# Loads that wait for a softmax, another way of joining float64 words, and a new step list

## The chip, the cores and the metric

The kernel runs on one core of one Trainium2 chip. The metric is the device time of one execution in microseconds (us). The core's engines are TensorE (PE, matmuls and transposes; its weight loads are PEld), VectorE (DVE), ScalarE (ACT), GpSimd (POOL), and SyncE (SP), which here issues every DMA.

## The reference

An attention over a small state is followed by two feed-forward layers. All inputs are float64 or float32 arrays as numpy draws them; the kernel is given the large weights as float64 words, which it makes into float32 itself.

```python
# x: 4 x 8 x 512 x 64, state: 4 x 8 x 32 x 64
a = softmax(x @ state^T / 8);   xread = a @ state
a2 = softmax(state @ x^T / 8);  sread = a2 @ x
x = concat(xread, sread)                       # 4 * 544 = 2176 tokens, 512 wide
x = (x @ w_a) * (x @ w_b) @ w_out              # 512 -> 1536 -> 512
h = x @ w_in                                   # 512 -> 2048
out = softplus(h) @ w_out2                     # 2048 -> 512, softplus = max(h,0) + log1p(exp(-|h|))
```

## The kernel before

The program is recorded first and placed afterwards. Each helper (`copy`, `tt`, `ts`, `stt`, `reduce`, `activation`, `transfer`, `Products`) adds a step to a `Plan`, with the engines that may run it and a cost for each. `Plan.run` reads the table `ORDER`, which gives steps their ranks; `Plan.go` then walks a model of the engines' time, takes for each engine that is free the first step by rank whose inputs are there, gives it places in the pools `F`, `R`, `K` (float32, float32r and PSUM tiles of 512 columns), and issues it. So the rank and the costs together set the order on every engine. Where TensorE would have a gap in that model during the first 60 us, `go` puts small matmuls on zeros into it (`warm`, line 572 of the profile); 14 such matmuls stand at the very start as well.

Attention comes first. Inputs `x` of batch b arrive in two DMAs of 512 KB (`load_x`), are transposed on TensorE (`turned`, line 560), and give scores against the state (`scores_of`, `scores_direct`). `state_softmax(b)` turns scores into weights over the 32 state rows. The first weights are not multiplied with `xread` but with the state first (`state_w`, `state_rows`): `gates_of(s, b)` then multiplies the softmax with that product for 256 columns of w_a and w_b (part s of six), and `y_part(s, b)` applies part s of w_out. The second feed-forward layer follows with `w_in`, softplus and `w_out2`.

A float32 product is carried on TensorE as three float32r products (`Products.three`): both operands are split into a high and a low part (`split_to`), one copy and one subtract each.

Weights arrive as float64 words and are joined to float32 in `convert_to`: `high` is the upper half of each word, `low` the lower one. Before the change this is one ACT and five DVE instructions on [128, 512] or [128, 1024] values: an ACT copy with a scale, a shift (`ts`), a join of the sign (`stt`), a mask that keeps the exponent (`ts`), the low half times that power of two (`stt`) and a float32 add (`tt`). `load_first` brings the first 256 columns of w_a and w_b in two halves each, `load_to` the later units in the order of the list `order`: `("wo", 0)`, `("ab", 1, 0)`, `("ab", 1, 2)`, `("wo", 1)` and so on. SP issues DMAs in program order, and one that waits holds those behind it.

Of the kernel before, what the change touches and what calls it, by code (L numbers as in the profile page):

```python
# [13 lines left out]
ALU = mybir.AluOpType  # L14
# [139 lines left out]


ORDER = """
1 0 3-4 6 18 5 7 17 30 10 19 13 29 20 8 31 22 9 32 21 33 12 23 214 34 11 24 215 14 35 59 25
60 216 61 39 217 37 2 62 38 69 40 16 26 63 15 36 41 133 28 70 64 91 27 42 71 43 47 134 72
128 44 92 45 73 46 65 79 48 129 67 135 80 49 81 136 50 89 68 82 137 126 51 138 74 90 52 55
53 66 75 54 127 83 139 57 77 56 84 108 93 76 130 140 78 109 85 131 58 94 110 156 96 95 111  # L160
87 157 141 100 86 112 142 97 143 98 113 88 132 114 101 144 116 99 102 115 117 103 145 172
118 104 146 106 173 185 147 107 186 119 183 174 236 120 184 190 175 233 121 187 122-123 237
176 188 150 189 124 158 234 258 191 259 125 247 177-178 162 159 179 192 163 193 260 160 248
261 194 149 151 238 168 165 195 161 264 219 196 201 249 164 218 166 105 240 152 197 167 265
154 182 180 155 153 235 198 220 304 250 181 170 199 171 227 207 262 200 202 239 251 290-291
263 335 252-254 242 228 241 208 221 306 203 307 224 204 223 209 222 225 293 305 210 243 205
255 206 169 244 256 309 266 308 245 294 232 336 211 267 310 229 257 270 311 337 268-269 230
212 246 296 275 213 297 322 321 338 271 226 312 272-274 339 298 276-277 313 315 340 379 314
278 284 341 299 350 316-318 343 300 319-320 279 380 342 371 351 302 324 468 280 325 285 292
301 281 344-345 352 148 372 282 353 469 373 303 382 295 358 286 381 354 374 287 357 327 385  # L170
288 329 355 386 328 470 331 347 383 356 360 346 384 330 323 471 417 333 361 363 387 348 472
366 375 473 407-408 231 401 364 477 367 289 326 332 349 475 418 283 334 376 410 402 478 474
404 359 362 476 498 479-482 365 483 409 405 499 377 388 411 368 378 415 500 462 369 505 403
370 501 406 392 446 433 432 502 506 389 412 438 390 413 439 503 419 393 414 395 435-436 396
441 463 391 504 586 464 442 434 587 448 536 588 449 537 440 451 423 443 420 428 397 444 421
589 445 590 422 452 429 465 579 425 437 484 430 416 485 595 585 431 487 591 596 399 398 488
507 426 454-455 394 427 450 447 457 453 594 490 400 597 491 424 466 510-511 494 512-513
598-599 516-518 458 519 493 526 486 527 529 467 530 523 600 524 520 489 460 508 534 461 509
495 538 496 616 541-543 615 514 497 547 551 532 580 593 552 521 554 456 581 555 622 539 560
617 563 561 531 557 565 623 558 568 533 569 571 573 572 574 583 525 540 546 515 618 566 582  # L180
703 556 492 619 528 559 553 522 562 535 575 459 564 620 545 621 592 601-602 548 604-605
607-608 577 610-611 640 567 576 584 570 654 578 549 544 550 704-705 629 609 733 624 603 606
627-628 630 709 706-707 634-635 651 637-638 708 612-613 643-644 625 646-647 614 712 669 626
641 653 713 671 642 658-661 668 714 655 664-667 645 672 639 715 675 674 677 734 633 678 716
710 631 735 682-683 686 685 739 691 688-689 649 717 692-693 696 648 632 656 736 699 676
701-702 680 650 670 737-738 657 770 652 711 694-695 662-663 673 679 718-732 697 684 681 687
636 740 690 698 741-769 700
"""


# [206 lines left out]
def attention_moe_moe2(ctx, tc, x, state, w_a, w_b, w_out, w_in, w_out2, out):  # L397
# [79 lines left out]
    def dve_us(n, wide):  # L477
        return 0.145 + (0.00105 if wide else 0.000527) * n

    def activation(o, i, func, **kw):  # L480
        also = [v for v in kw.values() if isinstance(v, Ref)]
        acc = [kw["accum_out"]] if "accum_out" in kw else []
        give = lambda: nc.scalar.activation(  # L483
            made(o), made(i), func, **{k: made(v) for k, v in kw.items()})
        plan.add({"act": (act_us(cols(o), in_psum(i)), give)}, [i, *also], [o, *acc])
# [7 lines left out]
        }  # L493
        plan.add(ways, [i], [o])

    def tt(o, a, b, op):
        n, ps = cols(o), in_psum(a, b)
        put = lambda eng: lambda: eng.tensor_tensor(  # L498
            out=made(o), in0=made(a), in1=made(b), op=op)
        ways = {"dve": (dve_us(n, True), put(nc.vector), *([] if ps else [True]))}  # L500
        plan.add(ways, [a, b], [o])

    def ts(o, i, s1, op0):
        give = lambda: nc.vector.tensor_scalar(made(o), made(i), s1, None, op0=op0)  # L504
        plan.add({"dve": (dve_us(cols(o), False), give, True)}, [i], [o])

    def stt(o, a, s, b, op0, op1):
        give = lambda: nc.vector.scalar_tensor_tensor(  # L508
            out=made(o), in0=made(a), scalar=s, in1=made(b), op0=op0, op1=op1)
        ps = in_psum(a, b)  # L510
        plan.add({"dve": (dve_us(cols(o), True), give, *([] if ps else [True]))}, [a, b], [o])
# [74 lines left out]

    raws = []

    def load(n, *srcs, act=False):

        b = Buf(F, 2 * n, RAW_SPARE)
        words = b.all().rearrange("p a b -> p (a b)").bitcast(U32)
        pairs = []
        for i, src in enumerate(srcs):
            src = src.rearrange("(k p) c -> p k c", p=P).bitcast(U32)
            dst = words.rearrange("p (k i c) -> p k i c", i=len(srcs), k=src.shape[1])
            pairs.append((dst[:, :, i, :], src))
        transfer(2 * n * W * P * 4, *pairs, act=act)
        return b
# [7 lines left out]
    def convert_to(v, b, spare=0):  # L607

        words = b.rearrange("p a b -> p (a b)").bitcast(U32)
        words = words.rearrange("p (c t) -> p c t", t=2)  # L610
        low, high = words[:, :, 0], words[:, :, 1]
        e = Buf(F, v.n, spare)
        v_, e_ = (i.rearrange("p a b -> p (a b)") for i in (v, e.all()))
        vu, eu = v_.bitcast(U32), e_.bitcast(U32)
        activation(v_, high.bitcast(F32), AF.Copy, scale=2.0 ** -112)
        ts(vu, vu, 3, ALU.logical_shift_left)
        stt(vu, high, 0x80000000, vu, ALU.bitwise_and, ALU.bitwise_or)
        ts(eu, vu, 0xFF800000, ALU.bitwise_and)
        stt(e_, low, 2.0 ** -52, e_, ALU.mult, ALU.mult)
        tt(v_, v_, e_, ALU.add)  # L620


    RAW_SPARE = 10
# [15 lines left out]
    def load_to(key):  # L639

        while key in order:
            k = order.pop(0)
            loaded[k] = load(*units[k])
# [23 lines left out]

    def load_x(b, g):

        if not g:  # L670
            xs[b] = Buf(X[b], KD)
        t = xs[b]
        transfer(2 * P * W * 4, (
            t.all(2 * g, 2).rearrange("p k (h w) -> p (k h) w", h=2),
            x[b, 4 * g:4 * g + 4].rearrange("h (p c) d -> p h (c d)", c=4)
        ))
        if not g:
            return

        if b < B - 1:  # L680
            t.then = lambda now: R.add(
                lambda: xp.tile([P, KD, W], F32R, tag=f"x{b}", name=f"xr{b}"), KD, now)
        else:
            t.then = lambda now: F.add(
                lambda: xp.tile([P, KD, W], F32, tag=f"x{b}", name="xf"), KD, now)
# [18 lines left out]
    load_first("b", 1)  # L704
    load_x(1, 0)
    load_x(1, 1)
    load_to(("wo", 0))
    load_x(2, 0)
    load_x(2, 1)
    load_to(("ab", 1, 0))  # L710
    load_x(3, 0)
    load_x(3, 1)

    def xn(b, p, c):

# [146 lines left out]
    def scores_direct(b, g0, n):  # L862
# [16 lines left out]
        m.end()  # L879
        return ps  # L880

    def state_softmax(b):

        e, whole = Buf(F, 2), Buf(F, 2) if b in G32 else None
        each = 1 if b in HALF else 2
        n = each * W // NS
        wide = lambda i: i[0][:, 0:n].rearrange("p (t n) -> p t n", n=1)
# [99 lines left out]
    def state_rows(s, p):  # L987
# [25 lines left out]
        for i in range(2):  # L1013
            both = Buf(R, 4, 4)
            split_to(banks[i].all(), both.all(0, 2), both.all(2, 2))
            for b in range(B):
                to = sw[s, b, p // 2]
                pairs = []
                for half in range(2):
                    q = 32 * quarter(b, 2 * i + half)  # L1020
                    src = both.all().rearrange("p (t i) c -> p i t c", i=2)
                    src = src[NS * b:NS * b + NS, half]
                    pairs.append((to.all()[q:q + NS].bitcast(F32), src.bitcast(F32)))
                transfer(2 * NS * 2 * W * 4, *pairs, us=0.63)

    def read_x(s):

# [137 lines left out]
        yparts[b] = lambda k, c0, n: tuple(v[:, k, c0:c0 + n] for v in views)  # L1165


    scores_of(0)
    bring_first("a", 0)
    state_w("a", 0)  # L1170
# [4 lines left out]
    state_w("a", 1)  # L1175
    bring_first("b", 1)
    state_w("b", 1)
    steps = [(s, b) for s in range(NHS) for b in range(B)]
    SREAD = 0
    pend = []  # L1180
# [178 lines left out]
```

## Time and profile before

| | |
|---|---|
| median of 3 runs | 735.6 us (735.36 to 735.81) |
| the profiled execution, its own time | 734.75 us |
| its span, first to last instruction | 733.0 us |
| PE busy | 726.5 us, 99% of the span |
| DVE busy | 608.2 us, 83% |
| ACT busy | 398.8 us, 54% |
| granted TensorE clock | 0.999, mean over the span |
| DMA moved | 66.20 MB, mean 90 GB/s |

The span begins with the first instruction and ends with the last. A busy time is the union of an engine's instructions. An instruction's length includes the tail of its pipeline, which overlaps the next one, so the distance between two starts is the cost of one in a row of them. A float32 matmul leaves two records in the trace, a float32r one leaves one.

### The profile page before, as it was taken

How to read it: one execution, taken by the hardware profiler on the slowest of the kernel's cores; microseconds unless marked ns; L12 is line 12 of the kernel's file. 1: busy time of each engine (PE TensorE's matmuls, PEld its weight loads, DVE VectorE, ACT ScalarE, POOL GpSimd, SP SyncE). 2: the span in 40 equal slices, each digit the busy share in tenths (PEclk: the TensorE clock that was granted, in tenths of full speed). 3: DMA queues.
4: the chain of work that ended last, by engine and by line, in shares of the span. 5: the costliest groups of instructions: out<-in, count | busy, mean ns of one | idle time of the engine just before them, and what ended most of it. 6: DMA issues, size and time to landing. Idle time of an engine off the chain costs nothing.

```text
span 733.0 us, 10298 instructions
## 1 busy us (share of the span) xinstructions
PE 726.5 (99%) x4090; PEld 602.4 (82%) x4090; DVE 608.2 (83%) x810; ACT 398.8 (54%) x643; POOL 0.7 (0%) x6
## 2 busy tenths in 40 slices
PE   9999999999999999999999999999999999999998
PEld 8577887778888877888888898888988889888897
DVE  7999999999597779799998778569887998886574
ACT  6878655234142323235685676654766657655570
POOL 0000000000000000000000000000000000000000
PEclk9999999999999999999999999999999999999999
DMA  9403791864546356733030001001020110101103
GB/s 308 168 1 130 214 242 48 210 172 107 145 114 173 73 158 149 197 114 116 1 114 1 1 0 59 1 0 58 1 93 24 58 31 28 59 0 59 58 1 129
DMA packets 35379, 66.20 MB, mean 90 GB/s; under 512 B 3716, under 2 KB 10116, under 8 KB 35332
## 3 DMA queue, kind: packets, MB, share of 16 engines
q1 hardware_dynamic: 35332, 65.55, 30.9%
q8 instruction: 32, 0.52, 0.3%
q14 instruction: 15, 0.12, 0.1%
HBM read 40.11 MB, written 4.46 MB: 61 GB/s over the span
## 4 chain that ended last, share of the span: by engine, by line
PE 95%; DVE 2%; ACT 2%; DMA 1%; issue 0%; SPq 0%; ACTq 0%
PE PS L545 93%; PE PS L560 2%; ACT SF L490 1%; ACT SF L483 1%; DVE SF L508 1%; DMA SF<-in_moe_w_a 1%; DVE SR L498 0%; DVE SF L498 0%; DVE SF L504 0%; DVE SM L514 0%; ACT SR L490 0%; SPq L525 0%; DVE SM L519 0%; DVE SM L504 0%; DVE SF L491 0%
## 5 line engine op out<-in xcount | busy, mean ns | idle before, releaser
L545 PE MATMUL PS<-SR 128*128 128x512 f32 (+3 forms) x2187 | 534.5, 377 | 1.2 <-DVE SR L662 1.2
L545 PEld LDWEIGHTS PS<-SR 128*128 128x128 f32 (+1 forms) x2187 | 386.2, 189 | 72.1 <-issue 2.2
L483 ACT ACTIVATE SF<-SF 128x512 f32<-128x512 f32 (+3 forms) x258 | 159.2, 629 | 23.9 <-DMA SF<-in_moe_w_b 10.6
L545 PE MATMUL PS<-SR,xr 128*128 128x512 f32 (+3 forms) x473 | 147.7, 386 | 0.0
L545 PE MATMUL PS<-xr,SR 128*128 128x512 f32 (+1 forms) x378 | 133.1, 391 | 0.0
L490 ACT CAST SR<-SF 128x1024 fp32r<-128x1024 f32 (+4 forms) x97 | 74.6, 772 | 106.4 <-DVE SF L498 104.8
L498 DVE TENSOR_TENSOR SF<-SF,PS 128x1024 f32<-128x1024 f32 (+3 forms) x118 | 108.7, 931 | 26.3 <-PE PS L545 25.5
L508 DVE SCALAR_TENSOR_TENSOR SF<-SF 128x512 f32<-128x512 f32 (+6 forms) x128 | 106.4, 834 | 0.8
L545 PEld LDWEIGHTS PS<-SR,xr 128*128 128x128 f32 x473 | 88.2, 188 | 18.2 <-issue 0.7
L498 DVE TENSOR_TENSOR SR<-SF,SR 128x1024 fp32r<-128x1024 f32 (+4 forms) x96 | 82.2, 862 | 16.1 <-ACT SR L490 15.5
L490 ACT COPY SF<-PS 128x1024 f32<-128x1024 f32 (+3 forms) x88 | 55.5, 663 | 56.4 <-PE PS L545 50.8
L545 PEld LDWEIGHTS PS<-xr,SR 128*128 128x128 f32 (+1 forms) x378 | 68.6, 187 | 15.1 <-issue 0.7
L508 DVE SCALAR_TENSOR_TENSOR SF<-PS,SF 128x512 f32<-128x512 f32 (+2 forms) x74 | 45.1, 609 | 43.1 <-ACT SF L483 43.0
L498 DVE TENSOR_TENSOR SF<-SF 128x512 f32<-128x512 f32 (+3 forms) x103 | 78.2, 761 | 1.6
L483 ACT ACTIVATE SF<-PS 128x512 f32<-128x512 f32 (+2 forms) x78 | 41.5, 532 | 39.7 <-PE PS L545 38.4
L504 DVE TENSOR_SCALAR SF<-SF 128x1024 uint32<-128x1024 uint32 (+1 forms) x61 | 39.4, 652 | 5.8 <-ACT SF L483 5.4
L545 PE MATMUL PS<-SF 64*32 64x128 f32 (+4 forms) x512 | 32.4, 321 | 1.5 <-issue 0.7
L490 ACT CAST SR<-PS 128x1024 fp32r<-128x1024 f32 (+2 forms) x27 | 22.9, 864 | 20.1 <-PE PS L545 11.2
L490 ACT CAST xr<-SF 128x1024 fp32r<-128x1024 f32 (+3 forms) x26 | 20.1, 772 | 25.0 <-DVE SF L498 24.9
L498 DVE TENSOR_TENSOR SR<-PS,SR 128x1024 fp32r<-128x1024 f32 (+2 forms) x29 | 30.1, 1043 | 1.6 <-ACT SR L490 1.3
L545 PEld LDWEIGHTS PS<-SF 64*32 64x32 f32 (+2 forms) x512 | 19.8, 127 | 10.0 <-issue 7.5
L545 PE MATMUL PS<-xr,xr 128*128 128x512 f32 x56 | 22.0, 396 | 0.0
(65 smaller groups left out, 292.1 us busy)
## 6 DMA issues: line engine op xcount, KB each, us to landing
SR<-SR SPq DMA_DIRECT2D x116, 128.0 KB, 2.4
SF<-in_moe_w_out SPq DMA_DIRECT2D x11, 1024.0 KB, 5.0
SF<-in_moe_w_in SPq DMA_DIRECT2D x7, 1024.0 KB, 5.2
SF<-in_moe_w_a SPq DMA_DIRECT2D x11, 512.0 KB, 4.6
SF<-in_moe_w_b SPq DMA_DIRECT2D x11, 512.0 KB, 6.1
xr<-SR SPq DMA_DIRECT2D x36, 128.0 KB, 2.4
x<-in_x SPq DMA_DIRECT2D x8, 512.0 KB, 9.1
out<-SF SPq DMA_DIRECT2D x14, 256.0 KB, 2.2
```

What stands on the lines that cost most here:

```text
L483: give = lambda: nc.scalar.activation(made(o), made(i), func, **{k: made(v) for k, v in kw.items()})
L490: "act": (act_us(n, ps), lambda: nc.scalar.copy(made(o), made(i))),
L498: put = lambda eng: lambda: eng.tensor_tensor(out=made(o), in0=made(a), in1=made(b), op=op)
L504: give = lambda: nc.vector.tensor_scalar(made(o), made(i), s1, None, op0=op0)
L508: give = lambda: nc.vector.scalar_tensor_tensor(out=made(o), in0=made(a), scalar=s, in1=made(b), op0=op0, op1=op1)
L545: self.all.append(lambda: nc.tensor.matmul(made(o), made(w), made(x), start=first, stop=last, **kw))
L560: self.all.append(lambda: nc.tensor.transpose(made(o), made(i), ident))
```

## The change

Four things change.

First, `load_last`, called after the first weights are joined, now creates the two loads of x of batch 3, and the loads of `("wo", 0)` and `("ab", 1, 0)`. Each target gets a tiny DVE memset that reads the last result of batch 0's state softmax (`weighed[0]`), so that the DMA into that target has to come after the softmax. The three later units aren't held: the list may bring them earlier.

Second, `convert_to` scales `low` by 2^-29 on ACT into an unsigned integer, which is then added to the joined high word as a 32-bit integer. In place of one ACT and five DVE instructions there are two ACT and three DVE instructions. The builder turns the integer add into an instruction that stands as ISA in the rows below and works on 16-bit halves: 1,024 of them for 512 values, 2,048 for 1,024.

Third, two costs in the plan's model: 0.25 us more for that add, and 1.7 times the bytes for the small SBUF-to-SBUF transfers in `state_rows`.

Fourth, `ORDER` is a new list for the steps of the whole program.

```diff
--- before.py
+++ after.py
@@ -154,37 +154,43 @@
 ORDER = """
-1 0 3-4 6 18 5 7 17 30 10 19 13 29 20 8 31 22 9 32 21 33 12 23 214 34 11 24 215 14 35 59 25
...
+2 0 15 1 13 5 3-4 6-8 12 10 14 22 11 9 16 23-24 17-18 210 25 211 27-28 26 43 212 42 54 29 56
+19 55 44 20 30 57 21 213 34 64 131 58 63 32 65 33 45 126 35 72 66 73 36 90 132-133 59 127 46
...
@@ -493,11 +499,11 @@
         }
         plan.add(ways, [i], [o])
 
-    def tt(o, a, b, op):
+    def tt(o, a, b, op, us=0.0):
         n, ps = cols(o), in_psum(a, b)
         put = lambda eng: lambda: eng.tensor_tensor(
             out=made(o), in0=made(a), in1=made(b), op=op)
-        ways = {"dve": (dve_us(n, True), put(nc.vector), *([] if ps else [True]))}
+        ways = {"dve": (us + dve_us(n, True), put(nc.vector), *([] if ps else [True]))}
         plan.add(ways, [a, b], [o])
 
     def ts(o, i, s1, op0):
@@ -586,9 +592,14 @@
 
     raws = []
 
+    held = []
+
     def load(n, *srcs, act=False):
 
         b = Buf(F, 2 * n, RAW_SPARE)
+        if held:
+            spot = b.all()[:, :, 0:1]
+            plan.add({"dve": (0.1, lambda: nc.vector.memset(made(spot), 0.0))}, held, [spot])
         words = b.all().rearrange("p a b -> p (a b)").bitcast(U32)
         pairs = []
         for i, src in enumerate(srcs):
@@ -613,11 +624,10 @@
         v_, e_ = (i.rearrange("p a b -> p (a b)") for i in (v, e.all()))
         vu, eu = v_.bitcast(U32), e_.bitcast(U32)
         activation(v_, high.bitcast(F32), AF.Copy, scale=2.0 ** -112)
+        activation(eu, low, AF.Copy, scale=2.0 ** -29)
         ts(vu, vu, 3, ALU.logical_shift_left)
         stt(vu, high, 0x80000000, vu, ALU.bitwise_and, ALU.bitwise_or)
-        ts(eu, vu, 0xFF800000, ALU.bitwise_and)
-        stt(e_, low, 2.0 ** -52, e_, ALU.mult, ALU.mult)
-        tt(v_, v_, e_, ALU.add)
+        tt(vu, vu, eu, ALU.add, us=0.25)
 
 
     RAW_SPARE = 10
@@ -667,7 +677,7 @@
 
     def load_x(b, g):
 
-        if not g:
+        if b not in xs:
             xs[b] = Buf(X[b], KD)
         t = xs[b]
         transfer(2 * P * W * 4, (
@@ -704,12 +714,8 @@
     load_first("b", 1)
     load_x(1, 0)
     load_x(1, 1)
-    load_to(("wo", 0))
     load_x(2, 0)
     load_x(2, 1)
-    load_to(("ab", 1, 0))
-    load_x(3, 0)
-    load_x(3, 1)
 
     def xn(b, p, c):
 
@@ -879,9 +885,12 @@
         m.end()
         return ps
 
+    weighed = []
+
     def state_softmax(b):
 
         e, whole = Buf(F, 2), Buf(F, 2) if b in G32 else None
+        weighed.append(e[1])
         each = 1 if b in HALF else 2
         n = each * W // NS
         wide = lambda i: i[0][:, 0:n].rearrange("p (t n) -> p t n", n=1)
@@ -1021,7 +1030,7 @@
                     src = both.all().rearrange("p (t i) c -> p i t c", i=2)
                     src = src[NS * b:NS * b + NS, half]
                     pairs.append((to.all()[q:q + NS].bitcast(F32), src.bitcast(F32)))
-                transfer(2 * NS * 2 * W * 4, *pairs, us=0.63)
+                transfer(3.4 * NS * 2 * W * 4, *pairs, us=0.63)
 
     def read_x(s):
 
@@ -1165,6 +1174,20 @@
         yparts[b] = lambda k, c0, n: tuple(v[:, k, c0:c0 + n] for v in views)
 
 
+    def load_last():
+
+
+        xs[3] = Buf(X[3], KD)
+        spot = xs[3].all()[:, 0:KD:2, 0:1]
+        plan.add({"dve": (0.07, lambda: nc.vector.memset(made(spot), 0.0))},
+                 [weighed[0]], [spot])
+        load_x(3, 0)
+        load_x(3, 1)
+        held.append(weighed[0])
+        load_to(("wo", 0))
+        load_to(("ab", 1, 0))
+        held.clear()
+
     scores_of(0)
     bring_first("a", 0)
     state_w("a", 0)
@@ -1175,6 +1198,7 @@
     state_w("a", 1)
     bring_first("b", 1)
     state_w("b", 1)
+    load_last()
     steps = [(s, b) for s in range(NHS) for b in range(B)]
     SREAD = 0
     pend = []
```

On SP the first loads stand in this order before (`x_79` is x of batch 0, `x_98` and `x_100` those of batches 1 and 2, `x_122` that of batch 3; 128x4x256 and 128x2x512 are 512 KB, 128x2x1024 is 1 MB):

```order
L525 DMA SF<-in_state 128x512
L525 DMA SF<-in_moe_w_a 128x4x256
L525 DMA x_79<-in_x 128x4x256
L525 DMA SF<-in_moe_w_b 128x4x256
L525 DMA x_79<-in_x 128x4x256
L525 DMA SF<-in_moe_w_a 128x4x256
L525 DMA x_98<-in_x 128x4x256
L525 DMA x_100<-in_x 128x4x256
L525 DMA SF<-in_moe_w_b 128x4x256
L525 DMA x_98<-in_x 128x4x256
L525 DMA x_100<-in_x 128x4x256
L525 DMA SF<-in_moe_w_out 128x2x1024
```

And in the changed kernel (`x_78` is batch 0, `x_103` batch 1, `x_99` batch 2, `x_449` batch 3):

```order
L531 DMA SF<-in_state 128x512
L531 DMA x_78<-in_x 128x4x256
L531 DMA SF<-in_moe_w_a 128x4x256
L531 DMA x_78<-in_x 128x4x256
L531 DMA SF<-in_moe_w_b 128x4x256
L531 DMA SF<-in_moe_w_a 128x4x256
L531 DMA SF<-in_moe_w_b 128x4x256
L531 DMA x_99<-in_x 128x4x256
L531 DMA x_103<-in_x 128x4x256
L531 DMA x_99<-in_x 128x4x256
L531 DMA x_103<-in_x 128x4x256
L531 DMA SF<-in_moe_w_a 128x2x512
```

The first half of x of batch 0 moves from the third to the second place and the second half from the fifth to the fourth; x of batches 1 and 2 starts one place later. The unit `("ab", 1, 2)` now follows x of batch 2, and `("wo", 0)`, which was twelfth, stands behind x of batch 3 and `("ab", 2, 0)`.

On PE the program begins like this before (128x32 are the direct scores of batch 0, 32x128 the products of `state_w`, 32x256 scores of batches 1 and 2, line 572 the small matmuls on zeros):

```order
L545 MATMUL PS<-SR 128x256 x14
L560 MATMUL PS<-ident,SF 128x128 x8
L572 MATMUL PS<-SR 128x256 x8
L560 MATMUL PS<-ident,x_79 128x128 x8
L572 MATMUL PS<-SR 128x256 x4
L545 MATMUL PS<-SF 32x128 x32
L545 MATMUL PS<-SF 128x32 x16
L560 MATMUL PS<-ident,x_79 128x128 x8
L545 MATMUL PS<-SF 32x256 x8
```

And now:

```order
L551 MATMUL PS<-SR 128x256 x14
L566 MATMUL PS<-ident,SF 128x128 x4
L566 MATMUL PS<-ident,x_78 128x128 x8
L566 MATMUL PS<-ident,SF 128x128 x4
L578 MATMUL PS<-SR 128x256 x7
L551 MATMUL PS<-SF 128x32 x16
L566 MATMUL PS<-ident,x_78 128x128 x8
L578 MATMUL PS<-SR 128x256 x6
L551 MATMUL PS<-SF 32x128 x32
L551 MATMUL PS<-SF 128x32 x16
L551 MATMUL PS<-SF 32x256 x8
```

The transposes of x stand between those of the state, the first direct scores come ahead of the first `state_w`, and the small matmuls stand at other places: 8, 4 and 4 before, 7, 6 and a later 4 now. The rest of TensorE's work is the same in number: 3,708 instructions before and 3,709 now, of which 16 and 17 are the small ones.

On DVE, at the place where the held loads are let go (the second memset of 128x4 is that of `("ab", 1, 0)`, the first that of `("wo", 0)`), the changed kernel has:

```order
L504 ISA SF<-SF 128x2048
L602 MEMSET SF 128x4
L504 TENSOR_TENSOR SF<-SF,PS 128x1024
L602 MEMSET SF 128x4
L504 TENSOR_TENSOR SR<-PS,SR 128x1024
L504 TENSOR_TENSOR SR<-SF,SR 128x1024 x2
L504 TENSOR_TENSOR SF<-SF,PS 128x1024
L510 TENSOR_SCALAR SF<-SF 128x1024
L497 CAST SR<-SF 128x1024
L514 SCALAR_TENSOR_TENSOR SF<-SF 128x1024
L504 TENSOR_TENSOR SR<-SF,SR 128x1024
L510 TENSOR_SCALAR SF<-SF 128x1024
```

The last row shown is the shift for `("wo", 0)`, and four rows further on stands the ISA that ends its joining. Before, there are no such memsets, and these two loads wait for DMA places alone.

## Rows read from the trace of the kernel before

**Rows 1.** Windows of the span: busy time of each engine, clock, DMA

```profile
0.00:30.00 30.00, 26.54 (x511) 22.54 (x512) 24.32 (x46) 22.58 (x36) 0.70 (x6) 1.00 0.87 291
30.00:60.00 30.00, 29.90 (x228) 19.57 (x227) 29.52 (x38) 23.23 (x40) 0.00 (x0) 1.00 0.03 6
60.00:733.00 673.00, 670.03 (x3355) 560.25 (x3353) 554.35 (x727) 353.01 (x568) 0.00 (x0) 1.00 0.30 85
```

**Rows 2.** Timeline of PE, first 30 us: start, length, instruction, idle before

```profile
4.34 1.41 PE L560 MATMUL PS<-ident,SF 128*128 128x128 f32 x8
5.50 1.20 PE L572 MATMUL PS<-SR 128*128 128x256 f32 x8
7.16 1.09 PE L560 MATMUL PS<-ident,x 128*128 128x128 f32 x8 [0.46 <-DMA x<-in_x]
8.01 0.72 PE L572 MATMUL PS<-SR 128*128 128x256 f32 x4
8.90 3.33 PE L545 MATMUL PS<-SF 64*32 64x128 f32 x96 [0.18 <-DVE SF L498]
12.17 1.09 PE L560 MATMUL PS<-ident,x 128*128 128x128 f32 x8
13.20 0.66 PE L545 MATMUL PS<-SF 64*32 64x256 f32 x16
13.79 1.09 PE L560 MATMUL PS<-ident,x 128*128 128x128 f32 x8
14.81 1.98 PE L545 MATMUL PS<-SF 64*128 64x32 f32 x32
16.72 1.09 PE L560 MATMUL PS<-ident,x 128*128 128x128 f32 x8
...
21.97 0.66 PE L560 MATMUL PS<-ident,SF 128*128 128x128 f32 x4 [0.39 <-ACT SF L490]
22.38 0.71 PE L572 MATMUL PS<-SR 128*128 128x256 f32 x4
...
24.98 1.96 PE L545 MATMUL PS<-SF 64*32 64x256 f32 x64
27.45 0.69 PE L545 MATMUL PS<-SF 64*32 64x128 f32 x29 [0.50 <-DVE SR L498]
28.88 1.47 PE L545 MATMUL PS<-SF 64*32 64x128 f32 x36 [0.74 <-issue]
```

**Rows 3.** Timeline of PE, the first work after that stretch

```profile
29.65 5.42 PE L545 MATMUL PS<-SF 128*128 128x512 f32 x12
```

**Rows 4.** Timeline of ACT: waits for the first, third and eighth 512 KB

```profile
4.97 0.68 ACT L483 ACTIVATE SF<-SF 128x512 f32<-128x512 f32 x1 [0.87 <-DMA SF<-in_moe_w_a]
...
8.62 0.69 ACT L483 ACTIVATE SF<-SF 128x512 f32<-128x512 f32 x1 [0.18 <-DMA SF<-in_moe_w_b]
...
16.79 0.69 ACT L483 ACTIVATE SF<-SF 128x512 f32<-128x512 f32 x1 [0.37 <-DMA SF<-in_moe_w_b]
```

**Rows 5.** Timeline of DVE: the kinds of instruction that conversions use

```profile
16.04 0.68 DVE L514 TENSOR_REDUCE SM<-SF 128x16 f32<-128x512 f32 x1
16.64 0.42 DVE L504 TENSOR_SCALAR SF<-SF 128x512 uint32<-128x512 uint32 x1
...
67.67 1.22 DVE L498 TENSOR_TENSOR SR<-PS,SR 128x1024 fp32r<-128x1024 f32 x1
68.81 0.68 DVE L504 TENSOR_SCALAR SF<-SF 128x1024 uint32<-128x1024 uint32 x1
69.41 1.22 DVE L498 TENSOR_TENSOR SR<-PS,SR 128x1024 fp32r<-128x1024 f32 x1
```

**Rows 6.** DMA issues by kind, KB each, median us to landing

```profile
SF<-in_moe_w_out SPq DMA_DIRECT2D x11, 1024.0 KB, 5.0
```

**Rows 7.** Timeline of PE in the second layer

```profile
501.60 3.34 PE L545 MATMUL PS<-SR 128*128 128x512 f32 x14
504.78 0.39 PE L545 MATMUL PS<-SR,xr 128*128 128x512 f32 x1
```

## What the change was forecast to do

> **What bounds the kernel now.** I read the windows first. From 60 us to the end TensorE is busy for 670.03 of 673.00 us at the full clock (1.00), and the 2.97 us that are missing are the end: the last subtract or add and the DMA out. From 30 to 60 us it lacks 0.10 us, in the first 30 us it lacks 3.46 [rows 1]. So from 30 us on nothing but TensorE's own work sets the time. That work has a fixed pace: 14 float32r products from 501.60 us to where the next one starts, 504.78, are 0.227 us each [rows 7]. The diff leaves their number as it is, so time can be won in the first 30 us alone, and it can be lost anywhere.
>
> Then I read TensorE's timeline for those 30 us, where idle time and the small matmuls on zeros (line 572) are both time without work [rows 2]. From 5.50 to 7.16 us it fills and waits for x of batch 0, 1.66 us. From 8.01 to 8.90 it fills and waits for a DVE add, 0.89. Then come 0.39 before 21.97, the fill of 0.71, 0.50 before 27.45 and 0.74 before 28.88. Together 4.89 us. The set of work done by then ends where the next instruction begins, at 29.65 us [rows 3].
>
> **The change part by part.**
>
> *x of batch 0 earlier.* The first 512 KB were taken at 4.97 us, the third at 8.62, the eighth at 16.79 [rows 4], and x's first half, the second one, at 7.16 [rows 2]. From the third to the eighth that is 1.63 us apiece. x of batch 0 now has places one and three, so 4.97 and 8.62. Both halves of w_a and w_b have places two, four, five and six: 7.16, about 10.2, 11.9 and 13.5. The halves of x of batches 1 and 2 have places seven to ten: about 15.2, 16.8, 18.4 and 20.1.
>
> I follow TensorE through the new order with start-to-start costs [rows 2]. Eight transposes cost 0.85 (7.16 to 8.01), or 1.02 where the tiling changes (13.79 to 14.81). Sixteen direct scores cost 1.91 (14.81 to 16.72). 32 products of `state_w` cost 1.36 (8.90 to 12.17 is 3.27 for these and 16 direct scores). Eight scores of batch 1 or 2 cost 0.59, 32 of them 1.96. On DVE 512 values cost 0.60, the shift of 512 at most 0.42, 1,024 values 1.14 and their shift 0.60 [rows 5].
>
> - 4.34: four state transposes, x's first half at 4.97, the other four, done at 6.4. ACT copies them (0.6), the scores could start at 7.0. Seven small matmuls at the 0.15 of before (1.20 for eight) last until 7.45: 1.05 us without work.
> - Scores until 9.36, x's second half until 10.36. `state_w` of w_a needs the joined words. From 7.0 DVE has a copy, a cast, a subtract, a shift, a sign join, a reduce and the integer sum in its way: four at 0.60, two at 0.42, the sum at 0.57, and 0.05 for each hand-over, which makes 11.2. So 0.9 without work.
> - `state_w`, scores, eight scores: 15.1. The seventh 512 KB is there at 15.2, the eighth at 16.8: 0.7 without work, then transposes until 17.7. DVE's next ten instructions end at 16.7, which is early enough.
> - `state_w`, eight scores, two times eight transposes, a copy that ACT has ready about 0.2 late, `state_w`, 32 scores, `state_w`, and eight transposes of the softmax: 27.2.
>
> The same set ended at 29.65: 2.45 us earlier. Counted the other way, 1.05 + 0.9 + 0.7 + 0.2 = 2.85 us without work stand against 4.89: 2.0 us. The two counts differ because groups that change tiling less often cost less. I take 2.2.
>
> *Four small matmuls later.* The fill of four now stands at about 39 us, where TensorE had no gap before [rows 1]. 4 x 0.15 = 0.6 us are lost. Against that stand six fewer changes between whole and tiled matmuls in the entire order; at (1.02 - 0.85) / 2 = 0.09 us that is 0.5, half of it in the walk already: 0.25 won.
>
> *The join.* Per [128, 1024] unit DVE loses a shift-like mask (0.60) and two instructions of 1.14 (product and add) and gets the integer sum. No row has that instruction. The shift, which has one source, gives 0.60 as the lower bound; twice the two-source row, since it counts 2,048 halves, gives 2.28 as the upper. Below nothing it can't be, as it writes every word. I take 1.14, the row of the float32 add that it replaces (same bytes, two sources), and half that for 512 values. DVE then saves 0.60 + 1.14 = 1.74 us in each of 32 large units, and ACT gets one more of about 1 us. None of it counts by itself: DVE's 554 busy us after 60 us stand beside a full TensorE [rows 1].
>
> The Trainium skill, "VectorE: DVE Perf Modes", section "Mode 2×_1P", says that two packed 16-bit values per port are taken each cycle even with two sources, provided a micro-op program for that mode exists. No run here has shown it. By that rule the sum costs what I took; where there is no such program it costs the upper bound, which is the slow rival below.
>
> *Held loads.* x of batch 3 is let go by DVE's 36th instruction, at about 25 us, and TensorE wants it after 24 transposes and six float32 products, past 35. w_out's first part is let go much later, and this is the tight place, since its first product follows. From the last transposes of batch 1's second round to that product TensorE has 62 float32r products (14.1), four float32 ones of four passes (3.6), 24 transposes (2.9), sixteen float32 ones of 128 columns (3.6), 96 small products (about 3.3, an estimate below `state_w`'s 1.36 per 32) and six small transposes (0.6): 28 us. DVE has from the same point to the last subtract of w_out's split 17 of 1.14, four shifts and one cast of 0.60, some 0.9 of small ones and three sums S: 23.3 + 3 S, with S = 1.14 26.7 us, so 1.3 us in hand. The DMA itself is no limit: 5.0 us to landing [rows 6] and one ACT pass are 6, and DVE has 9.9 us of other work between the release and its first instruction on w_out. 88 products later (20 us) DVE needs 14.1 + 4 S more: 45.4 against 48, 2.6 in hand. In this I put down nothing. On SP the loads for the later parts and the transfers of `state_rows` stand behind the held ones; their users stand over 20 us further on in TensorE's order, so I count nothing for them either.
>
> **Sum.** -2.2 + 0.6 - 0.25 = -1.85 us. The profiled execution took 734.75 us (span 733.0), so 732.9 for one like it. It lay 0.85 under the median of the runs, 735.6, so against that median I forecast 733.8 us.
>
> **Rivals.**
>
> *The gain stays in the beginning.* DVE was busy for 29.52 of 30 us from 30 to 60 us [rows 1]. If hand-overs between engines cost 0.1 more than I put in, over the dozen steps of the walk, 1 us of the 1.85 goes: 734.8, which can't be told from no change. For it speaks that three fills with 17 small matmuls still stand in the order, where there were three with 16; against it, that x's wait of 1.66 us goes by the queue order alone.
>
> *The slow sum.* If the integer sum takes the 16-bit halves one by one (S = 2.28), the chain to w_out's first product needs 30.1 us against 28, and by the seventh sum 53.4 against 48: TensorE stands 5.4 us. The beginning wins 1.1 us less too. -0.75 + 5.4 = +4.7: 740.3 us. At S = 1.5 DVE has nothing in hand; from about 1.8 on (50.0 against 48) the loss is greater than what is won. For it speaks that the operands are 16 bits wide and twice as many; against it, that a chunk of the same bytes took 1.14.
>
> *More than I count.* If the small matmuls end in time and the sum is at its lower bound, the fills cost nothing and the first walk's 2.45 hold with 0.5 more from the two joins: -3.2, 732.4 us.
>
> **How the numbers follow.** 1.5 us is about 0.2% and what a measurement can tell from no change. Forecast and the case with more: 0.53 together (0.43 and 0.10), with a range of 732.2 to 734.1. The gain that stays in the beginning: 0.29, from 734.1 to 737.1. The slow sum: 0.18, from 737.1 to 740.3. So faster 0.53, same 0.29, slower 0.18. For 8 in 10 I go from 732.0 to 737.2: below lies under 0.05, above about 0.15.
>
> **What would show it.** In the changed profile TensorE's wait for x at 7.16 should be gone, the transposes of x stand near 5.0, and the first float32 product of 512 columns begins near 28.9 (after 16 more transposes). ISA of 2,048 should read about 1.2 us, and PE should show no wait for DVE after 60 us. A PE wait for DVE's split of w_out near 75 to 100 us would prove the slow sum or a late release; PE waits for ACT in the first 30 us would prove the first rival.

## The result, and the profile after

The changed kernel takes 745.7 us (median of 4 executions, 745.04 to 747.05), the kernel before 735.5 (735.31 to 735.81): a ratio of 1.0139, with a 95% interval of 1.0127 to 1.0152. That is 10.2 us slower, outside the range of the forecast. The profiled execution took 745.04 us, with a span of 743.3. One of the four executions of e3 below, the profiled one, took 812.52 us at a mean granted clock of 0.851 and is left out of the figures; e5 is the same kernel, profiled again.

The line of busy time on the page of after, and the windows that answer to [rows 1], with the third of them in four pieces:

```profile
PE 730.6 (98%) x4091; PEld 604.2 (81%) x4091; DVE 549.4 (74%) x746; ACT 432.2 (58%) x674; POOL 0.7 (0%) x6
```

```profile
0.00:30.00 30.00, 26.53 (x516) 23.06 (x517) 22.23 (x41) 22.97 (x41) 0.70 (x6) 1.00 0.78 256
30.00:60.00 30.00, 29.66 (x353) 19.62 (x352) 28.87 (x44) 25.14 (x49) 0.00 (x0) 1.00 0.11 37
60.00:150.00 90.00, 90.00 (x495) 72.67 (x494) 73.27 (x77) 57.73 (x70) 0.00 (x0) 1.00 0.65 187
150.00:236.00 86.00, 84.69 (x389) 66.89 (x388) 59.09 (x57) 34.34 (x37) 0.00 (x0) 1.00 0.52 129
236.00:252.00 16.00, 11.37 (x39) 8.82 (x38) 6.67 (x7) 4.16 (x4) 0.00 (x0) 0.79 0.43 99
252.00:743.00 491.00, 488.30 (x2308) 413.14 (x2306) 359.28 (x524) 287.87 (x476) 0.00 (x0) 1.00 0.19 57
```

The first 60 us look as before, and so do the next 90 and the last 491 with the usual end. In the 16 us from 236 to 252 TensorE lacks 4.63 us of work, and the mean clock there is 0.79; from 150 to 236 it lacks 1.31. So TensorE, which had nothing to wait for there, now waits for others. For whom is in its waits, by who ended them (total, times, longest; the first three):

```profile
PE PS L551 <- DVE SR L504: 4.8, 2, 4.6
PE PS L551 <- DVE SR L672: 1.2, 1, 1.2
PE PS L551 <- issue: 1.1, 2, 0.7
```

One wait of 4.6 us stands out. On PE's timeline it lies at 240 us:

```profile
239.54 0.39 PE L551 MATMUL PS<-SR,xr 128*128 128x512 f32 x1
244.56 2.50 PE L551 MATMUL PS<-SR,xr 128*128 128x512 f32 x5 [4.63 <-DVE SR L504]
```

The chain of waits shows what came in between (start, length, what):

```profile
227.92 11.80 PE PS L551 x52
...
239.81 1.23 DVE SF L504
241.04 0.02 issue
241.06 1.05 ACT SR L496
242.12 0.03 issue
242.14 2.37 DVE SR L504 x2
244.51 0.04 issue
244.56 7.47 PE PS L551 x20
```

The product that waits is the first of `read_y` of part 3, and it wants the low half of w_out's fourth part, which is the second of the two subtracts at 242.14. That subtract takes no result of the three steps ahead of it in the chain; it stands behind them on DVE. They are the last multiply of the same part's gates, its copy to float32r on ACT and its own subtract, and the multiply can only start when TensorE has done the last gate product, at 239.8. The place of the float32r pool that the plan gives to the low half was itself read by the gate products just ahead of the wait. With this place the subtract could have gone ahead of those three steps, but not ahead of these products. So TensorE stands for 4.6 us while DVE and ACT go through 3.5 us of other work that is queued ahead of a 1.2-us subtract.

Behind the wait comes a second loss. The clock in windows around it:

```profile
239.50:243.40 3.90, 0.43 (x2) 0.01 (x1) 2.48 (x3) 1.46 (x2) 0.00 (x0) 1.00 0.56 129
243.40:250.20 6.80, 5.64 (x13) 4.46 (x14) 1.79 (x2) 0.63 (x1) 0.00 (x0) 0.50 0.69 159
250.20:257.00 6.80, 6.80 (x31) 5.59 (x30) 2.75 (x3) 0.00 (x0) 0.00 (x0) 1.00 0.00 0
```

After 3.5 us without work the granted clock falls to 0.50, the 1.2 GHz level, and stays there for 6.8 us, of which TensorE works 5.64: 13 products at 0.434 us instead of the 0.227 of [rows 7]. That is 13 x 0.207 = 2.7 us more. With the 4.6 of the wait, the 1.3 that are lacking from 150 to 236 us and 0.2 more from 30 to 60 us (29.66 against 29.90) this makes 8.8 of the 10.2 us; where the rest lies isn't shown.

### The profile page after: what moved, and what is told of

Its sections match the earlier page's. It is cut to its first block, busy times and chain, and to the rows that moved or that the text cites. A ratio compares the mean times of both kernels' runs of the same rounds, so it can differ in the third digit from the quotient of the medians.

```text
span 743.3 us, 10292 instructions
## 1 busy us (share of the span) xinstructions
PE 730.6 (98%) x4091; PEld 604.2 (81%) x4091; DVE 549.4 (74%) x746; ACT 432.2 (58%) x674; POOL 0.7 (0%) x6
## 3 DMA queue, kind: packets, MB, share of 16 engines
HBM read 40.11 MB, written 4.46 MB: 60 GB/s over the span
## 4 chain that ended last, share of the span: by engine, by line
PE 94%; DMA 2%; DVE 2%; SPq 1%; issue 1%; ACT 1%; DVEq 0%; ACTq 0%
PE PS L551 91%; PE PS L566 2%; DMA x<-in_x 1%; SPq L531 1%; DVE SR L504 1%; DMA xr<-SR 1%; DVE xr L504 0%; DVE SF L504 0%; ACT SF L496 0%; ACT SR L496 0%; DVE SF L514 0%; DVE xf L504 0%; PE PS L578 0%; DVEq L504 0%; ACTq L496 0%
## 5 line engine op out<-in xcount | busy, mean ns | idle before, releaser
L551 PE MATMUL PS<-SR 128*128 128x512 f32 (+3 forms) x2014 | 515.1, 382 | 2.3 <-DVE SR L672 1.2
L551 PEld LDWEIGHTS PS<-SR 128*128 128x128 f32 (+1 forms) x2014 | 364.2, 189 | 74.5 <-issue 2.8
L551 PE MATMUL PS<-SR,xr 128*128 128x512 f32 (+2 forms) x690 | 196.9, 373 | 4.8 <-DVE SR L504 4.8
L489 ACT ACTIVATE SF<-SF 128x512 f32<-128x512 f32 (+5 forms) x254 | 175.1, 709 | 11.2 <-DMA SF<-in_moe_w_b 5.7
L551 PEld LDWEIGHTS PS<-SR,xr 128*128 128x128 f32 x690 | 126.6, 189 | 27.0 <-DVE SR L504 5.6
L551 PE MATMUL PS<-xr,SR 128*128 128x512 f32 (+2 forms) x332 | 112.0, 392 | 0.0
L504 DVE TENSOR_TENSOR SR<-SF,SR 128x512 fp32r<-128x512 f32 (+4 forms) x97 | 81.8, 849 | 20.3 <-ACT SR L496 19.7
L514 DVE SCALAR_TENSOR_TENSOR SF<-SF 128x1024 uint32<-128x1024 uint32 (+4 forms) x90 | 73.1, 814 | 0.4
L504 DVE CUSTOM_DVE_ANT_0 SF<-SF 128x2048 uint16<-128x2048 uint16 (+1 forms) x34 | 39.3, 1157 | 2.6 <-ACT SF L489 1.5
L504 DVE TENSOR_TENSOR SF<-SF 128x512 f32<-128x512 f32 (+2 forms) x56 | 33.9, 604 | 0.9
```

The costliest lines, as they stand in the source:

```text
L489: give = lambda: nc.scalar.activation(made(o), made(i), func, **{k: made(v) for k, v in kw.items()})
L504: put = lambda eng: lambda: eng.tensor_tensor(out=made(o), in0=made(a), in1=made(b), op=op)
L514: give = lambda: nc.vector.scalar_tensor_tensor(out=made(o), in0=made(a), scalar=s, in1=made(b), op0=op0, op1=op1)
L551: self.all.append(lambda: nc.tensor.matmul(made(o), made(w), made(x), start=first, stop=last, **kw))
```

## The experiments

The kernel before ran beside each group of these on the same chip, with medians of 735.62 (e1 to e4), 735.65 (e5 to e8) and 735.52 us (e9, e10). The changed kernel itself did not; its 745.7 us were measured beside the 735.5 above.

**e1: the list alone.** Step 582 of the list is that subtract.

```diff
-547 640 581 520 608 ... 644 702 582 632 669
+547 640 581 582 520 608 ... 644 702 632 669
```

> The changed kernel with one step moved in the list: the subtract that makes the low half of w_out's fourth part now stands right behind the copy that makes the high half (it stood 119 places later). Theory A (that subtract comes late, TensorE stands 4.6 us for it, and its clock is at half speed for 6.8 us right after): the 4.6 us wait near 240 us is gone, the granted clock stays at full speed throughout, and the time falls by 4.6 + 3.4 = 8 us to about 737.7; waits of 0.3 to 0.8 us at other places stay. Theory B (the loads held back by the softmax, or the new form of joining words, make the kernel late everywhere): at most the one wait goes and comes back elsewhere, 742 us or more.

737.98 us, ratio 1.0033 [1.0020, 1.0045], as theory A has it: 7.7 us are back by one subtract that stands 23 instructions earlier on DVE. The clock is 1.00 throughout. PE's waits of e1:

```profile
PE PS L550 <- DVE SF L503: 1.2, 4, 0.5
PE PS L550 <- DVE SR L671: 1.2, 1, 1.2
PE PS L550 <- issue: 0.8, 2, 0.5
```

The 4.8 for `DVE SR` are gone. What is left above before, 2.4 us, are small waits like those of after, which this one move doesn't touch.

**e2: the planner's transfer cost alone undone.**

```diff
-                transfer(3.4 * NS * 2 * W * 4, *pairs, us=0.63)
+                transfer(2 * NS * 2 * W * 4, *pairs, us=0.63)
```

> The changed kernel with one cost of the plan's model undone: the small transfers are priced at their bytes again, not 1.7 times them. Theory A, with the reason that the model keeps places of the float32r pool for transfers that it prices too long, so that the subtract of w_out gets its place late: the 4.6 us wait and the slow clock go, about 737 us. Theory A without that reason (the list's rank alone): the wait stays, about 745. Theory B: 745 as well.

735.24 us, ratio 0.9996 [0.9987, 1.0005]. All of the loss is gone with one number that no instruction carries; of theory A the form with the reason holds, and the time is lower than the 737 that it gave. The transfers on the chip are the same; the planner believes that they hold their places in the float32r pool for longer, so a tile that is to take such a place is planned later, and the steps that write it with it.

The planner's model of time, which is no measurement, says so itself when `Plan.go` is worked through for each kernel. In the changed kernel the subtract of the low half could start at 163.1 us and is given no place until 256.6, when the second of two such transfers ends. TensorE is idle in the model for 13.4 us ahead of this very `read_y` (244.5 to 257.9), and the program ends at 758.8 us, against 737.0 for the kernel before. With the old cost the place comes at 226.4, there is no gap there, and the end is 739.8. So the loss could be read from the plan before a run, though not its size.

The rest of the change, which is new joins, earlier x, held loads and a new list, is worth nothing that can be measured.

**e8: the same number in the kernel before.**

```diff
-                transfer(2 * NS * 2 * W * 4, *pairs, us=0.63)
+                transfer(3.4 * NS * 2 * W * 4, *pairs, us=0.63)
```

> The kernel before with one edit: the cost of the transfers of state_rows in the planner 3.4 instead of 2. It says whether that cost harms by itself or only with the new list. Theory A (only together: with the old list no split that TensorE waits for loses its place): 735.6, within 1 us, no wait over 1 us after 60 us. Theory B (the cost harms any list, as places of the fp32r pool are held longer in the plan): 737 or more, with a TensorE wait for a DVE subtract between 150 and 260 us.

744.25 us, ratio 1.0117 [1.0100, 1.0135]: the number costs 8.6 us with the old list and the old joins too, so theory B holds: it doesn't need the new list to do harm. (A list can still take most of the harm away, as e1 shows.) PE's timeline:

```profile
169.82 0.93 PE L545 MATMUL PS<-SR 128*128 128x512 f32 x3 [2.74 <-DMA SR<-SR]
...
174.88 1.65 PE L545 MATMUL PS<-SR,xr 128*128 128x512 f32 x3 [2.75 <-DVE SR L498]
```

And the clock behind the second wait:

```profile
174.90:182.00 7.10, 7.10 (x24) 5.67 (x25) 2.19 (x2) 1.01 (x1) 0.00 (x0) 0.77 0.74 168
```

It is a loss of the same kind at another place: TensorE stands for a transfer and for a subtract, and after two waits with 2.3 us of work between them the mean clock of the next 7.1 us is 0.77. What the subtract stands behind on DVE is another thing here: the chain of waits runs through a load of w_b that lands at 167.3 us and its joining on ACT and DVE, and the subtract starts at 173.6.

**e3 and e5: the wait filled.** 42 small products on zeros stand ahead of `read_y` of part 3, with a planned cost of nothing, so that everything else keeps its order.

```diff
+        for _ in range(42 if s == 3 else 0):
+            m.one(ps[0][:, 0:HW], blank[:, 0:P], blank, True, True, us=0.0)
```

> The changed kernel with 42 matmuls on zeros (128x256, 0.12 us each) put in front of the product that waits near 240 us; nothing else moves. If the half-speed clock after the wait comes from TensorE having stood idle: the wait is as long as before, filled, the granted clock stays at full speed, and 3.4 us come back, 742.3 us. If the clock falls for another reason at that place (the transfers, the work before it): the half-speed stretch stays and the time is 745 to 746.

741.94 us (median of the other three executions), ratio 1.0081 [1.0064, 1.0099], so 3.8 us under after, where 3.4 were expected.

> The kernel of e3 once more (42 products on zeros in the place of the wait at about 240 us), for its profile. Theory of the clock: the granted clock reads 1.00 in the stretch from 243 to 251 us, where the changed kernel read about 0.5, and the products behind the wait stand 0.227 us apart instead of 0.43; the span is about 3.4 us under that of the changed kernel, near 740 us. Rival (something else slows these products, for example their operands): they stay 0.43 us apart.

742.23 us in one execution, with a span of 740.4. The first two windows of before in e5:

```profile
239.50:243.40 3.90, 3.90 (x34) 3.90 (x34) 2.79 (x3) 1.79 (x2) 0.00 (x0) 1.00 0.64 146
243.40:250.20 6.80, 6.80 (x36) 5.76 (x35) 2.68 (x3) 0.31 (x1) 0.00 (x0) 1.00 0.65 149
```

And the products behind the filled wait:

```profile
244.25 1.55 PE L551 MATMUL PS<-SR,xr 128*128 128x512 f32 x6
245.63 6.74 PE L551 MATMUL PS<-SR 128*128 128x512 f32 x29
```

The real work starts at 244.25 where after has 244.56, so it waits about as long. With TensorE kept busy the clock stays at 1.00, and six products behind the wait take 1.38 us to the next start, 0.23 apiece. So the theory of the clock holds. Its price is 2.7 us as worked out above, 2.9 between the two profiled spans (743.3 and 740.4) and 3.8 between the medians: about 3 of the 10.2 us.

**e4: the join alone.** Before, with its list and its planned costs, but the three last joining steps exchanged. The order of before is kept by a detour: the ACT pass is entered in the plan as the DVE mask that it replaces, at the mask's place and with its cost, behind the sign join (`vu`); and a step that does nothing stands for the product. In the change the pass is planned as ACT work and needs `low` alone.

```diff
-        ts(eu, vu, 0xFF800000, ALU.bitwise_and)
-        stt(e_, low, 2.0 ** -52, e_, ALU.mult, ALU.mult)
-        tt(v_, v_, e_, ALU.add)
+        n = cols(eu)
+        plan.add({"dve": (dve_us(n, False), lambda: nc.scalar.activation(
+            made(eu), made(low), AF.Copy, scale=2.0 ** -29), True)}, [low, vu], [eu])
+        plan.add({"dve": (dve_us(n, True), lambda: None, True)}, [low, e_], [e_])
+        tt(vu, vu, eu, ALU.add)
```

> The kernel before with the new way of joining words alone: in the same order on every engine, the mask becomes an ACT instruction, the product is left out, the float add becomes the integer add. Theory A: TensorE is full as before, 735.5 us, 1 us to either side. Theory B (the new join costs time through ACT or through the integer add): 738 us or more, with TensorE waiting for ACT or DVE in the first 180 us.

736.83 us, ratio 1.0025 [1.0013, 1.0038]: slower by 1.2 us, between the two theories, although DVE is busy 551.5 us where it was 608.2. PE's longest wait of e4 for another engine's work, and the window that answers to the second of [rows 1]:

```profile
56.10 1.98 PE L545 MATMUL PS<-SF 128*128 128x512 f32 x4 [1.27 <-ACT SF L490]
```

```profile
30.00:60.00 30.00, 28.36 (x223) 18.68 (x222) 25.94 (x34) 24.15 (x41) 0.00 (x0) 1.00 0.01 1
```

ACT has one more pass per unit, and at 54.8 us TensorE now waits for it, where before it lacked 0.10 us in the whole window. ACT is idle for a fifth of this window and still late at one place. This is the price of a pass that the plan doesn't know to be ACT's; in e2, whose plan does, the new join goes with no loss that can be measured.

**e7: x of batch 3 not held** (with e2's cost).

```diff
-                 [weighed[0]], [spot])
+                 [], [spot])
-11 9 16 ... 138 81 254 99 31 83 97 ... 78 82 116
+11 9 81 83 82 16 ... 138 254 99 31 97 ... 78 116
```

> The changed kernel with the transfer cost of before (e2), and x of batch 3 not held: its two loads stand right behind those of batches 1 and 2 and wait for nothing of batch 0's softmax. The prediction put down nothing for the hold. Theory (the hold costs and gains nothing, as x of batch 3 is there at about 31 us and wanted at 36.4): 735.2, within 0.5 us of e2, and the first 60 us as busy as in e2 (55.6 us). Rival (early loads of x take the queue from the weights that follow, or take a place that others need): TensorE waits for a load or a split between 20 and 60 us, 1 us or more, 736.3 or more.

737.8 us, ratio 1.0028 [1.0015, 1.0042], 2.6 above e2. So loads of x of batch 3 that are issued right behind those of batches 1 and 2 cost time. The edit takes the hold away and moves the loads in the list, both at once; what the hold alone is worth, with the loads at their place, isn't shown. The time is the rival's, but the wait is earlier than it has it. PE's timeline of e7:

```profile
18.95 1.07 PE L565 MATMUL PS<-ident,x 128*128 128x128 f32 x8 [1.72 <-DMA x<-in_x]
```

And in e2:

```profile
17.49 1.06 PE L566 MATMUL PS<-ident,x 128*128 128x128 f32 x8 [0.45 <-ACT SF L496]
```

The transposes that wait for x's second landing for batches 1 and 2 start at 18.95, where e2 has 17.49. (ACT starts on the first half of w_a at 8.58 in e7 and at 8.40 in e2, so a late landing of that transfer, of which e10 below tells, isn't the difference.) The two transfers of x of batch 3 are now issued right behind these; that they take part of their bandwidth is the likely cause and was not tried by itself. Nor is it settled how the 2.6 us divide between this wait and the rest of the first 30 us.

**e6, e10 and e9: the beginning.** In e2's profile TensorE stood 1.27 us before 24.69 us for the low half of a `state_w`, which DVE ends at 24.27 behind a reduce. e6 moves that step:

```diff
-38 136 125 76 68 ... 77 62 129
+38 136 125 62 76 68 ... 77 129
```

> The changed kernel with the transfer cost of before (e2) and one DVE step, the low half of a state_w of batches 2 and 3, moved ahead of an integer sum and of a reduce of 1.21 us of batch 0's softmax. In e2's trace TensorE stands from 23.42 to 24.69 us, 1.27 us, until that step ends at 24.27. Theory (that step's place on DVE ends the wait): the wait is gone, and the time is 1.2 us under e2's 735.24, about 734.0, ratio to before 0.998. Rival (TensorE waits a little later for the sum or the reduce that the step was moved past): the idle time moves to between 24 and 30 us, and the time stays within 0.4 us of 735.2.

735.31 us, ratio 1.0000 [0.9991, 1.0009]. The wait is gone in the trace, and the time is that of e2, as the rival has it. e10 shows a part of the reason:

> The kernel of e2 once more, for its profile: the profiled execution of e2 was its longest (736.27 against a median of 735.24). If the wait of 1.27 us before 24.69 us belongs to the kernel, it stands here too, and the first product of 512 columns starts at 31.3 us again; if it came in that execution alone, the wait is under 0.5 us, and that product starts about 1 us earlier, as in e6.

735.19 us. The wait is 0.52 us here, between what the two cases were to show, and the product starts 1.05 us earlier. PE's timeline of e10:

```profile
7.37 1.98 PE L551 MATMUL PS<-SF 64*128 64x32 f32 x32
...
11.44 3.94 PE L551 MATMUL PS<-SF 64*32 64x128 f32 x112 [0.37 <-DVE SF L504]
15.31 1.09 PE L566 MATMUL PS<-ident,x 128*128 128x128 f32 x8
16.67 1.06 PE L566 MATMUL PS<-ident,x 128*128 128x128 f32 x8 [0.26 <-DMA x<-in_x]
...
23.36 3.18 PE L551 MATMUL PS<-SF 64*32 64x128 f32 x127 [0.52 <-issue]
26.93 0.69 PE L551 MATMUL PS<-SF 64*32 64x128 f32 x23 [0.39 <-issue]
27.55 2.84 PE L566 MATMUL PS<-ident,SF 128*128 128x128 f32 x24
30.22 3.17 PE L551 MATMUL PS<-SF 128*128 128x512 f32 x7
...
40.11 0.73 PE L578 MATMUL PS<-SR 128*128 128x256 f32 x4 [0.21 <-ACT SF L496]
40.68 1.03 PE L566 MATMUL PS<-ident,SF 128*128 128x128 f32 x8
```

On DVE two subtracts of low halves end near the ends of the waits of 0.52 and 0.39 us, at 23.37 and 26.66:

```profile
22.74 0.63 DVE L504 TENSOR_TENSOR SR<-PS,SR 128x512 fp32r<-128x512 f32 x1
25.98 0.68 DVE L504 TENSOR_TENSOR SR<-PS,SR 128x512 fp32r<-128x512 f32 x1
```

In e2's profile, its longest execution (736.27), the row of 30.22, the first products of 512 columns, starts at 31.27. The two profiles part at ACT's wait for the first half of w_a, 8.40 us in e2:

```profile
8.40 1.25 ACT L489 ACTIVATE SF<-SF 128x512 f32<-128x512 f32 x2 [0.70 <-DMA SF<-in_moe_w_a]
```

and 7.54 in e10:

```profile
7.54 1.23 ACT L489 ACTIVATE SF<-SF 128x512 f32<-128x512 f32 x2 [0.31 <-DMA SF<-in_moe_w_a]
```

So the beginning of one and the same program differs by 1 us between two executions, and the wait that e6 takes away is less than half as long in the other one. In e6's profile that landing is late too (ACT starts at 8.32), and the product of 512 columns starts at 29.84: the moved step helps there, but over eleven executions the medians don't differ. e9 goes on from e6 and issues the first loads of x of batches 2 and 1 (not both of batch 1, as the expectation has it) ahead of the second half of w_b:

```diff
-3-4 6-8 12 10 14 ... 35 72 66 73 36 ... 46 91 67
+3-4 6-7 12 10 8 14 ... 35 66 36 ... 46 91 72 73 67
```

> The kernel of e6, and in the list the two loads of x of batch 1 ahead of the second half of w_b, whose two ACT passes come later. In e6's trace TensorE goes through the transposes of x of batch 1 at 16.10 and 17.65 us as the loads land, with about 0.4 and 0.7 us idle ahead of them; the load that is put back is wanted by DVE at about 19 us only. Theory (the order of the landings ends these two waits): the transposes start at about 15.5 and 16.4 us, and the products of 512 columns 1.1 us earlier, at about 28.7 instead of 29.84; the time is 734.2 against 735.3, ratio to before about 0.998. Rival (ACT and DVE, both full here, are late instead, as w_b's join comes later): the wait moves to the products between 18 and 27 us, and the time stays within 0.4 us of 735.3.

735.98 us, ratio 1.0003 [0.9994, 1.0012]. The rival's mechanism was right, and the time lies 0.3 us above its band; PE's timeline of e9:

```profile
15.45 2.22 PE L565 MATMUL PS<-ident,x 128*128 128x128 f32 x16
18.38 1.94 PE L550 MATMUL PS<-SF 64*32 64x128 f32 x80 [0.70 <-DVE SF L503]
```

The transposes no longer wait for a landing, and the products behind them wait for DVE instead. No kernel of this study beats the one before by more than the measurement can tell; e2 is the nearest.

## Why the prediction was wrong, by its steps

- **What bounds it.** Right for before, and the sentence that time "can be lost anywhere" was the right warning. It was not followed up: the working then looks for losses at w_out's first part and 88 products behind it only.
- **The step that failed: the end of "Held loads", "I count nothing for them either".** The sum checks w_out's first part, near 75 to 100 us, and there it was right: PE is busy for all of the 90 us from 60 to 150 in after. Then the loads for the later parts and the transfers of `state_rows` are let off with "their users stand over 20 us further on in TensorE's order". That looks at TensorE's order, not at DVE's, nor at the places that those transfers hold in the plan. The wait is for w_out's fourth part, and it comes from the place of its subtract behind the gates. The edit that put it there, 2 to 3.4 in the transfer cost, has no term in the prediction at all: no row prices a number in a planner, and the planner's own gap of 13.4 us was not looked at. In its place the runs show 10.5 us (745.7 to e2's 735.24) with the new list, 8.6 with the old (e8).
- **A price that was missing even so.** The rivals count an idle TensorE by the length of its wait. Here 4.6 us of waiting brought about 3 more by the clock (e3, e5).
- **x earlier, -2.2 us.** The mechanism was right, the size was not. Without the loss further on (e10) the walk's points come as follows: the first scores at 7.37 (walk 7.45), `state_w` at 11.44 (11.2), the first transposes of batches 2 and 1 done at 17.7 (17.7). Its last ten microseconds were too short: the set of work was to end at 27.2 and ends at 30.22 less the 1.75 of the 16 more transposes, 28.5. Two waits of 0.52 and 0.39 us near the ends of DVE's subtracts of low halves are 0.9 of the 1.3, though the rows name no releaser for them; the walk priced DVE's chain up to `state_w` of w_a in detail and the later ones as early enough. So -1.2 against the 29.65 of [rows 3], and -0.6 in after, where the products of 512 columns start at 30.82.
- **The integer sum.** Right: S was taken as 1.14, the pitch of a two-source float32 instruction over the same bytes, which reads 1.22 busy in [rows 5]. The group of after reads the same for twice as many values of half the size:

```profile
L504 DVE CUSTOM_DVE_ANT_0 SF<-SF 128x2048 uint16<-128x2048 uint16 x30 | 36.6, 1220 | 2.5 <-ACT SF L489 1.5
```

The Trainium skill, "VectorE: DVE Perf Modes", section "Mode 2×_1P", describes two packed 16-bit values per cycle for two sources, and the trace agrees in the time. Whether the instruction runs in that mode, no run here shows. The slow sum is out.
- **The join costs nothing by itself.** Half right. DVE's 58.8 us (608.2 to 549.4) bring nothing, as said. But e4 shows that the extra ACT pass costs 1.2 us in the old order, which wasn't planned for it; "ACT gets one more of about 1 us" was left without a price. In the new order no such loss is left (e2).
- **x of batch 3 held, nothing.** Not settled: e2, with the hold, stands level with before, and no run takes the hold away alone. e7 does show that the place of these loads matters, 2.6 us; the prediction asked when x of batch 3 is wanted, not whom its transfer would slow.
- **Gain stays in the beginning** (734.8) is what the change without its planner number does: 735.24 against a forecast of 733.8. Of the 1.2 us won at the start the later fill takes most: its four small products stand at 40.11 in e10 and last 0.57 us to the next start, as forecast, with 0.21 idle ahead of them. The 0.4 that is left is what the medians show (735.62 to 735.24), but the interval of that ratio is wider, and no run leaves the fill out.

## What to carry to other kernels

A cost in a planner is an edit of the program: before anything else, look in the planner's own time for gaps of the bound engine that the old number didn't have, follow on each engine which instructions the new number moves, and for each product that waits, see what stands ahead of its operand's last writer on that writer's engine, down to the last repetition of the pattern and not the first alone. When a forecast says that the bound engine stays full, the loss from one broken place can be larger than the wait, because the clock may fall behind it. And a gain of 1 us in the beginning is hard to see where one landing moves by as much between two executions.

## What was not expected of the hardware

- TensorE's granted clock fell to 0.50 after 3.5 us without work in the middle of a run that was otherwise full, and came back 6.8 us later. Products on zeros in the wait kept it at 1.00 and gave about 3 us back (e3, e5).
- The landing of the first half of w_a, the third transfer of the program, was seen at 7.5 and at 8.4 us in two executions of one program (e10, e2).
- With two more transfers issued behind the loads of x of batches 1 and 2, the transposes that need the second of these started at 18.95 us, 1.5 us later than in e2 (e7, one profile of each).
